# ScalarE in program order during the prologue, and w_in's magnitudes on VectorE, in a sigmoid-attention and MLP kernel

## The chip, the core and the metric

The kernel runs on one core of a Trainium2 chip. A core has five engines, each with an instruction stream of its own: TensorE (PE, matrix products; its weight loads are shown apart as PEld), VectorE (DVE), ScalarE (ACT), GpSimd (POOL) and SyncE (SP, which here only starts DMAs). An engine does its stream strictly in order; streams meet at semaphores. Data lies in SBUF (128 partitions), matrix products end in PSUM.

The metric is the time on the device of one execution, in microseconds (us). A profiled execution leaves a trace, with the begin and end of each instruction.

## The reference

```python
def _attn_ref(q, k, v):                      # each (8, 12, 448, 64), f32
    S = q.shape[2]
    scale = 1.0 / np.sqrt(q.shape[-1])
    scores = scale * np.matmul(q, k.transpose(0, 1, 3, 2)) - np.log(S)
    attn = 1.0 / (1.0 + np.exp(-scores))
    return np.matmul(attn, v).astype(np.float32)

def _moe_ref(x, w_in, w_out):                # (3584, 768) @ (768, 2048) @ (2048, 768)
    h = x @ w_in
    neg, pos = h <= -1.0, h >= 1.0
    g = np.where(pos, h, np.where(neg, 0.0, (h + 1.0) ** 2 / 4.0))
    return (g @ w_out).astype(np.float32)
```

The output of attention is put into x: one row for each of the 8 x 448 positions, 12 heads x 64 columns. Each weight of attention is a sigmoid by itself; there is no sum over a row.

## The kernel before

**Units of work.** A batch of 448 positions has 12 heads, taken two at a time: six pairs of heads a batch, 48 in all. A pair is four pieces, three of 128 key positions and a short one of 64, so a batch of attention is 24 pieces. `step(i)` does piece i: `scores` (products of k and q, L407 in the form of pairs 0 to 7), `weigh` (the sigmoid on ScalarE, L454 in batch 0 and 1, L457 later) and `av` (product with v, L498), which lags by three pieces. At the end of a pair ScalarE copies its x out of PSUM (L504) and VectorE takes the largest magnitude (L508).

**Number formats.** Products run in fp16, with each operand as a high and a low half and three products in place of one; a power of two, found from the largest magnitude, scales each operand first. Pairs 0 to 7 are an exception: they are used in f32 as they come. From pair 8 on, `load_pair` fetches a pair into one of two `raw` buffers, `prep_a` finds its largest magnitudes, and `prep_b` makes the scales and the halves. Up to pair 46 (`MAX_ACT = 47`) `prep_a` runs on ScalarE, three Abs passes that keep a sum (L344); after it on VectorE, two reductions (L346). Up to pair 16 (`QA = 17`) the halves come from ScalarE and VectorE (L373, L374), after it from GpSimd (L378 and the lines behind it).

**Weights.** w_in and w_out are 16 chunks of 128 rows each. They arrive as 64-bit words, whose bits `Weight.convert` turns into f32. For a chunk f these are, in order: an Abs pass on ScalarE (L224); the magnitudes; then on VectorE two shifts (L241), the low bits (L244) and the sign (L247). With chunk f's Abs go VectorE's lines for chunk f - 1 and, where a sum is used, the sum for chunk f - 2. Magnitudes come in two ways. For a chunk in `summed` (in w_in every second one) the values are only clamped (L226; on GpSimd below chunk 7, on VectorE from there), and ScalarE sums the converted chunk (L218). For the others VectorE clamps and keeps the largest value in one instruction (L236). w_in's raw words lie in room of w_out_sb until they are used, and the next load is issued from SP once a chunk is converted.

After chunks 0 to 7 `find_scale` makes w_in's first scale: a reduction, one product on TensorE that brings the largest value to all partitions (L175), and a few small instructions ending at L135 and L139 (in `scales`). `split` then makes the fp16 halves: high on ScalarE (L286), low on VectorE (L287). The halves of chunk f lie where the f32 values of chunk f - 1 were, so L286 of a chunk overwrites what L287 of the chunk before reads.

**Stages.** (1) The prologue: attention of batch 0 piece by piece, with the conversion of w_in woven in: 9 conversion steps by piece `WI_A = 14`, the rest after it. There the first scale is found and chunks 0 and 1 are split. Loads of pairs 8 and 9 are issued at pieces 9 and 12 (`L0`, `LSTEP`), their magnitudes at pieces 19 and 22 (`A0`). (2) `finish_x(0)`: the scale of batch 0's x and its halves, L521 and L522. (3) The up products of batch 0 (`ups`, L722, with `bend` at L735 to L739), half of its down products (L758), attention of batch 1, and the conversion of w_out. (4) Batch 1, in which w_in is also put together into blocks for a seven-product scheme (`mix`). (5) Batches 2 to 7: `ups_blocks` (L688), then `downs`, and in between attention of the next batch. An up phase and a down phase make one batch.

**What sets the order.** A scheduler sorts the instructions of each engine by a simulated timeline and by priority, in `high_priority` blocks earlier. An engine named in `manual_schedule` is left out of that: it takes its work in the order in which the program is written. Before, this holds for SP in the prologue's loop alone.

Of the kernel before, what the change touches and what calls it, by code (L numbers as in the profile page):

```python
# [14 lines left out]
F32 = mybir.dt.float32  # L15
# [3 lines left out]
AF = mybir.ActivationFunctionType  # L19
ALU = mybir.AluOpType  # L20
# [3 lines left out]
P = 128  # L24
# [12 lines left out]
NA = 8  # L37
AHEAD = 2
LAST = 84
LAST1 = 18  # L40
WI_A = 14
WI_B = 5
WO_A = 42
WO_B = 66
# [24 lines left out]

PM = 9  # L70
WI_PRIO = 280
X_PRIO = 593


@with_exitstack
def sigmoid_attention_mlp(ctx: ExitStack, tc: tile.TileContext, first_qvk, qkv, w_in, w_out, out_t):
    nc = tc.nc
    NFULL, _, _, S = first_qvk.shape
    B = out_t.shape[1] // S
    NFC, _, DM = w_out.shape  # L80
# [6 lines left out]
    GROUPS = slice(0, NA), slice(NA, NFC)  # L87
# [7 lines left out]
    out_p = ctx.enter_context(tc.tile_pool(name="outp", bufs=2))  # L95
# [4 lines left out]
    ps_mo = ctx.enter_context(tc.tile_pool(name="ps_mo", bufs=3, space=PSUM))  # L100
# [78 lines left out]
    class Weight:  # L179


        def __init__(self, dram, sb, name, spare):
            self.dram, self.sb, self.name, self.spare = dram.bitcast(I32), sb, name, spare
            self.words, self.at, self.loaded = {}, 0, 0
            self.scale, self.inv = [], []
            self.most = const.tile([P, 2, NFC], F32, name=name + "_most")
            nc.vector.memset(self.most, 0.0)
            mod = WI_SUM if name == "wi" else WO_SUM
            self.summed = [f for f in range(NFC) if mod and f % mod == 0 and f not in (NA - 1, NFC - 1)]

        def f32(self, f):
            return self.sb[:, f + 1].rearrange("p h n -> p (h n)").bitcast(F32)
# [16 lines left out]

        def convert(self):  # L210

            f = self.at - 2
            if 0 <= f < NFC:
                w = self.words.pop(f)
                if f in self.summed:

                    dump = wo.f32(-1) if self is wi else w[:, :DM].bitcast(F32)
                    nc.scalar.activation(dump, self.f32(f), AF.Abs, accum_out=self.most[:, 1, f : f + 1])  # L218
                if self is wo:
                    self.load(3 if f == 3 else 1)  # L220
            f = self.at
            if f < NFC:
                a = self.f32(f)
                nc.scalar.activation(a, self.words_of(f)[1].bitcast(F32), AF.Abs)  # L224
                if f in self.summed:
                    (nc.vector if f >= CLAMP else nc.gpsimd).tensor_scalar(  # L226
                        out=a, in0=a, scalar1=HIGH_MIN, scalar2=None, op0=ALU.max
                    )
            f = self.at - 1
            if 0 <= f < NFC:  # L230

                low, high = self.words_of(f)
                a = self.f32(f)
                ai = a.bitcast(I32)
                if f not in self.summed:
                    nc.vector.tensor_scalar(  # L236
                        out=a, in0=a, scalar1=HIGH_MIN, scalar2=0.0, op0=ALU.max, op1=ALU.max,
                        accum_out=self.most[:, 0, f : f + 1],
                    )

                nc.vector.tensor_scalar(  # L241
                    out=ai, in0=ai, scalar1=5, scalar2=2, op0=ALU.logical_shift_left, op1=ALU.logical_shift_right
                )
                nc.vector.scalar_tensor_tensor(  # L244
                    out=ai, in0=low, scalar=29, in1=ai, op0=ALU.logical_shift_right, op1=ALU.bitwise_or
                )
                nc.vector.scalar_tensor_tensor(  # L247
                    out=ai, in0=high, scalar=-0x40000000, in1=ai, op0=ALU.bitwise_and, op1=ALU.bitwise_or
                )
# [376 lines left out]
    def mix(i):  # L626
# [87 lines left out]
    hold = {}  # L714
# [28 lines left out]
    def down(b, m, u, k):  # L743

        lo, hi = (0, NFC) if k is None else (GROUPS[k].start, GROUPS[k].stop)
        if u == 0:
            hold["po"] = ps_mo.tile([P, 512], F32, tag="mo", name="po")
            hold["o"] = out_p.tile([P, S], F32, tag="o", name="o")
            if m == 0:
                hold["od"] = down_sc[b, k]()  # L750
            if k == 1:
                nc.sync.dma_start(out=hold["o"], in_=part[m])
        po, o = hold["po"], hold["o"]

        pair = (u, u + NFC // 2) if b >= SB else (lo + 2 * u, lo + 2 * u + 1)
        for f in pair:
# [137 lines left out]
    for b in range(1, B):  # L894
# [6 lines left out]
        first = at  # L901
# [65 lines left out]
```

## Time and the profile before

| | |
|---|---|
| three runs | 1194.42, 1192.86, 1188.74 us; median 1192.86 |
| profiled execution | 1187.38 us |
| its span in the trace, first to last instruction | 1185.7 us |
| busy in the span: PE, DVE, ACT, POOL | 1144.9, 854.9, 697.6, 332.8 us |
| first scale of w_in ready | 47.9 us |
| scale of batch 0's x ready | 90.0 us |
| first up product | 91.7 us |
| one batch from batch 2 on, from one first up product to the next | 137.2 us |

How to read it: a row of the timeline has its start and its duration in us, the engine, the line of the program, what is written from what, and in brackets how long the engine stood idle before, with what released it. A group's row has the busy time of its instructions, the mean duration of one in ns, and that idle time summed. A stretch's row (windows) has, for each engine, the busy time within the stretch and the number of instructions.

### The profile page before, as it was taken

Reading aid. Unit: us, or ns where it says so; the run is one execution under the profiler, and the core shown is the slowest. Engines: PE = TensorE matmul, PEld = TensorE weight load, DVE = VectorE, ACT = ScalarE, POOL = GpSimd, SP = SyncE. Lnnn points to the kernel's source line nnn. Section 1 sums busy time; section 2 is a strip of 40 time slices with the busy share of each in tenths; the row PEclk is TensorE's granted clock in tenths of the full one; section 3 lists DMA queues with packets and bytes.
Section 4 is the critical chain, followed back from the end, with each engine's and each line's share of the span. In section 5 each row is a group of like instructions: output and inputs, shape, how many; then the busy total and the mean of one; then the engine's idle time right before and its main releaser. Section 6 shows DMA issues by size and latency. Waiting matters only on the chain.

```text
span 1185.7 us, 20268 instructions
## 1 busy us (share of the span) xinstructions
PE 1144.9 (97%) x7662; PEld 669.3 (56%) x7662; DVE 854.9 (72%) x1828; ACT 697.6 (59%) x1158; POOL 332.8 (28%) x393
## 2 busy tenths in 40 slices
PE   5889899999999999999999999999999999999998
PEld 1224333444445776457754677557764577558954
DVE  6999999999956588457973689456884678736830
ACT  5886576665654577547864578455864476613510
POOL 3004410011323244234345235332532353310000
PEclk9899999999999999999999999999999999999999
DMA  9842354437542266224643065423552246302400
GB/s 367 322 153 76 118 161 152 134 119 257 182 148 72 95 217 210 76 72 142 238 163 102 30 236 208 135 64 128 204 211 64 65 147 220 126 24 87 163 16 32
DMA packets 58113, 170.01 MB, mean 143 GB/s; under 512 B 8608, under 2 KB 39840, under 8 KB 51872
## 3 DMA queue, kind: packets, MB, share of 16 engines
q1 hardware_dynamic: 56288, 159.29, 39.1%
q10 hardware_dynamic: 1728, 9.44, 2.2%
q8 instruction: 60, 0.98, 0.3%
q14 instruction: 37, 0.30, 0.1%
HBM read 126.94 MB, written 23.40 MB: 127 GB/s over the span
## 4 chain that ended last, share of the span: by engine, by line
PE 71%; DVE 17%; DMA 4%; ACT 3%; issue 2%; POOL 2%; SPq 0%; POOLq 0%; ACTq 0%; DVEq 0%
PE po L758 33%; PE ph L688 22%; PE pav L498 8%; PE psc L416 3%; PE psc L425 2%; PE ph L722 2%; DVE g L736 2%; PE psc L411 1%; DVE g L737 1%; DVE ghl L739 1%; DMA raw<-qkv 1%; DVE ahl L466 1%; DVE w_in_sb L244 1%; DVE mixa L632 1%; DVE w_out_sb L247 1%
## 5 line engine op out<-in xcount | busy, mean ns | idle before, releaser
L758 PE MATMUL po<-ghl,w_out_sb 128*128 128x448 f16 x2304 | 446.3, 353 | 1.5 <-DVE qkv_e L131 0.6
L758 PEld LDWEIGHTS <-w_out_sb 128*128 128x128 f16 x2304 | 221.7, 98 | 219.4 <-issue 15.9
L688 PE MATMUL ph<-w_in_sb 128*128 128x224 f16 x3024 | 307.7, 259 | 1.3 <-DVE g L737 0.9
L688 PEld LDWEIGHTS <-w_in_sb 128*128 128x128 f16 x3024 | 282.6, 98 | 30.1 <-issue 27.2
L466 DVE SCALAR_TENSOR_TENSOR ahl<-psc,ahl 128x896 f16<-128x896 f32 (+1 forms) x170 | 153.0, 900 | 105.7 <-ACT ahl L465 103.6
L378 POOL TENSOR_SCALAR raw<-raw,qkv_s 128x448 f32<-128x448 f32 (+1 forms) x93 | 71.0, 777 | 449.9 <-DVE qkv_i L139 346.3
L457 ACT ACTIVATE psc<-psc,nls,sqk 128x896 f32<-128x896 f32 (+1 forms) x136 | 129.5, 971 | 103.5 <-PE psc L425 86.6
L465 ACT ACTIVATE ahl<-psc 128x896 f16<-128x896 f32 (+1 forms) x170 | 126.9, 762 | 29.8 <-DVE ahl L466 28.6
L722 PE MATMUL ph<-xhl,w_in_sb 128*128 128x448 f16 x576 | 114.5, 356 | 4.7 <-DVE g L737 3.4
L344 ACT ACTIVATE dump<-raw 128x448 f16<-128x448 f32 (+1 forms) x105 | 61.9, 589 | 85.8 <-DMA raw<-qkv 84.5
L697 DVE TENSOR_TENSOR xhl<-ph,xhl 128x224 f32<-128x224 f32 x240 | 87.7, 383 | 25.3 <-PE ph L688 19.4
L738 ACT ACTIVATE ghl<-g 128x448 f16<-128x448 f32 x128 | 72.5, 573 | 44.2 <-DVE g L737 43.8
L498 PE MATMUL pav<-ahl,v 128*64 128x448 f16 x748 | 95.6, 360 | 0.0
L735 ACT ACTIVATE g<-xhl,hr,ihr 128x448 f32<-128x448 f32 x96 | 68.7, 752 | 41.9 <-DVE xhl L697 41.0
L722 PEld LDWEIGHTS <-w_in_sb 128*128 128x128 f16 x576 | 55.7, 99 | 63.6 <-issue 14.4
L736 DVE SCALAR_TENSOR_TENSOR g<-g,rk 128x448 f32<-128x448 f32 x112 | 81.4, 741 | 10.2 <-ACT g L735 10.0
L739 DVE TENSOR_TENSOR ghl<-g,ghl 128x448 f16<-128x448 f32 x128 | 85.0, 672 | 5.3 <-ACT ghl L738 4.8
L768 DVE TENSOR_SCALAR o<-po,od 128x448 f32<-128x448 f32 x48 | 32.5, 679 | 61.1 <-PE po L758 60.8
L380 POOL TENSOR_TENSOR hl<-raw,hl 128x448 f16<-128x448 f32 x62 | 71.1, 1167 | 0.0
L416 PE MATMUL psc<-qk 128*128 128x448 f16 x252 | 66.3, 354 | 2.0 <-ACT a L454 1.0
L737 DVE SCALAR_TENSOR_TENSOR g<-xhl,ihs,g 128x448 f32<-128x448 f32 x96 | 66.3, 708 | 0.3
L498 PEld LDWEIGHTS <-v 128*64 128x64 f16 x748 | 36.3, 109 | 37.9 <-issue 23.0
(167 smaller groups left out, 1198.5 us busy)
## 6 DMA issues: line engine op xcount, KB each, us to landing
w_in_sb<-blocks SPq DMA_DIRECT2D x48, 1344.0 KB, 6.1
raw<-qkv SPq DMA_DIRECT2D x34, 704.0 KB, 4.7
qk<-hl SPq DMA_DIRECT2D x320, 56.0 KB, 2.0
w_out_sb<-w_in SPq DMA_DIRECT2D x16, 768.0 KB, 8.5
out_t<-o SPq DMA_DIRECT2D x48, 224.0 KB, 1.9
blocks<-mixs SPq DMA_DIRECT2D x8, 768.0 KB, 3.5
w_out_sb<-w_out ACTq DMA_DIRECT2D x6, 768.0 KB, 4.1
raww<-w_out ACTq DMA_DIRECT2D x6, 768.0 KB, 5.7
```

Of the source, the lines that this page charges most:

```text
L416: nc.tensor.matmul(out, kq[:, j, 1, w], kq[:, j, 0, :], start=True, stop=False)
L457: nc.scalar.activation(a, a, AF.Sigmoid, bias=nls, scale=sqk)
L465: nc.scalar.activation(hi, x, AF.Copy, scale=ATT)
L466: nc.vector.scalar_tensor_tensor(out=lo, in0=x, scalar=ATT, in1=hi, op0=ALU.mult, op1=ALU.subtract)
L498: nc.tensor.matmul(pav[j * D : (j + 1) * D, :S], *terms[j][t], start=c == 0 and t == 0, stop=mid and t == len(terms[j]) - 1,)
L688: nc.tensor.matmul(out, w[:, wt, wh, c * P : (c + 1) * P], xc[:, xt, c, xh, :], start=j in (0, 2) and c + wh + xh == 0, stop=c == HC - 1 a ...
L697: add = lambda out, q, other: nc.vector.tensor_tensor(out=out, in0=quarter(q), in1=other, op=ALU.add)
L722: nc.tensor.matmul(ph[:, :S], w_in_sb[:, f, wh, c * P : (c + 1) * P], xhl[:, c, xh, :], start=c == 0 and wh + xh == 0, stop=c == NCC - 1 a ...
L736: nc.vector.scalar_tensor_tensor(out=g, in0=g, scalar=rt, in1=g, op0=ALU.min, op1=ALU.mult)
L737: nc.vector.scalar_tensor_tensor(out=g, in0=h, scalar=ihs, in1=g, op0=ALU.mult, op1=ALU.max)
L739: (nc.gpsimd if f % GPOOL else nc.vector).tensor_tensor(out=ghl[:, f, 1, :], in0=g, in1=hi, op=ALU.subtract)
L758: nc.tensor.matmul(po[:, :S], w_out_sb[:, f, wh, m * P : (m + 1) * P], ghl[:, f, gh, :], start=f == lo and wh + gh == 0, stop=f == hi - 1 ...
```

## The change

It consists of constants and a few lines:

- `AM = 1`: in the prologue's loop ScalarE, too, takes its work in program order.
- `WI_SUM = 0`: `summed` is empty. The 8 sums on ScalarE (L218) and the 8 clamps (L226, four on GpSimd and four on VectorE) are gone; L236, now L240, runs on all 16 chunks of w_in. `CLAMP` and `SLAG` then have nothing to act on.
- `WI_A = 11`: the first nine conversion steps are spread over 11 pieces instead of 14, and the scale of w_in and the first two splits come after piece 11.
- `MAX_ACT = 20`: the magnitudes of pairs 20 to 46 come from VectorE (now L350, two instructions a pair) instead of ScalarE (three).
- `QA = 20`: the halves of pairs 17 to 19 are made by ScalarE and VectorE instead of GpSimd.
- `L0 = 10`, `LSTEP = 1`: loads of pairs 8 and 9 at pieces 10 and 11, magnitudes at 19 and 20.
- `X_PRIO = 600`: a priority, for `finish_x(0)`.
- `MIXA = 0`, `CUT = 8` and the keys of `hold`: new switches, left where they give the instructions and the order of before.

Lines of the program move by three or four (L135 becomes L138, L454 becomes L458), behind `mix` by seven (L722 becomes L729).

```diff
-WI_A = 14
+WI_A = 11
-WI_SUM = 2
-WO_SUM = 0
-MAX_ACT = 47
-L0 = 9
+WI_SUM = 0
+MAX_ACT = 20
+L0 = 10
-LSTEP = 3
+LSTEP = 1
-CLAMP = 7
-QA = 17
+CLAMP = 2
+QA = 20
+SLAG = 2
+AM = 1
+MIXA = 0
+CUT = 8
-X_PRIO = 593
+X_PRIO = 600
...
-            mod = WI_SUM if name == "wi" else WO_SUM
-            self.summed = [f for f in range(NFC) if mod and f % mod == 0 and f not in (NA - 1, NFC - 1)]
+            mod = WI_SUM if name == "wi" else 0
+            early = [f for g in GROUPS for f in range(g.start, g.stop - SLAG + 1)]
+            self.summed = [f for f in early if mod and f % mod == 0]
...
+            f = self.at - SLAG
+            if 0 <= f < NFC and f in self.summed:
+                nc.scalar.activation(wo.f32(-1), self.f32(f), AF.Abs, accum_out=self.most[:, 1, f : f + 1])
             f = self.at - 2
             if 0 <= f < NFC:
-                w = self.words.pop(f)
-                if f in self.summed:
-                    dump = wo.f32(-1) if self is wi else w[:, :DM].bitcast(F32)
-                    nc.scalar.activation(dump, self.f32(f), AF.Abs, accum_out=self.most[:, 1, f : f + 1])
+                self.words.pop(f)
...
-    with tc.manual_schedule(engines={mybir.EngineType.SP}):
+    with tc.manual_schedule(engines={mybir.EngineType.SP} | ({mybir.EngineType.Activation} if AM else set())):
```

Some instructions move with this. The first place is the start of ScalarE's stream. `a_123` and the other a are sigmoids of batch 0's pieces in turn, `w_in_sb<-w_out_sb` is the Abs of a chunk of w_in. Before:

```order
L224 ACT_TABLE_LOAD
L224 ACTIVATE w_in_sb<-w_out_sb 128x768
L454 ACT_TABLE_LOAD
L454 ACTIVATE a_123<-psc,nls 128x896
L454 ACTIVATE a_128<-psc,nls 128x896
L224 ACTIVATE w_in_sb<-w_out_sb 128x768
L218 ACTIVATE w_out_sb,wi_most<-w_in_sb 128x768
L224 ACTIVATE w_in_sb<-w_out_sb 128x768
L454 ACTIVATE a_133<-psc,nls 128x896
L454 ACTIVATE a_140<-psc,nls 128x448
```

ScalarE in the changed kernel, from its start:

```order
L458 ACT_TABLE_LOAD
L458 ACTIVATE a_123<-psc,nls 128x896
L458 ACTIVATE a_128<-psc,nls 128x896
L458 ACTIVATE a_133<-psc,nls 128x896
L458 ACTIVATE a_140<-psc,nls 128x448
L458 ACTIVATE a_149<-psc,nls 128x896
L228 ACTIVATE w_in_sb<-w_out_sb 128x768
L458 ACTIVATE a_157<-psc,nls 128x896
L228 ACTIVATE w_in_sb<-w_out_sb 128x768
```

The first Abs stands behind five sigmoids instead of ahead of all, and one table load is gone with it.

The second place is VectorE behind w_in's first scale (`wi_s`, and its inverse `wi_i`). L287, now L291, is the low half of a split; L236, now L240, the largest value; L241 and L244, now L245 and L248, belong to the conversion. Before:

```order
L135 TENSOR_SCALAR wi_s<-wi_e 128x1
L139 TENSOR_SCALAR wi_i<-wi_e 128x1
L135 TENSOR_SCALAR qkv_s<-qkv_e 128x2
L139 TENSOR_SCALAR qkv_i<-qkv_e 128x2
L156 CAST mb<-m_447 128x2
L241 TENSOR_SCALAR w_in_sb<-w_in_sb 128x768
L360 TENSOR_SCALAR sqk<-qkv_i 128x1
L244 SCALAR_TENSOR_TENSOR w_in_sb<-w_out_sb,w_in_sb 128x768
L247 SCALAR_TENSOR_TENSOR w_in_sb<-w_out_sb,w_in_sb 128x768
L287 SCALAR_TENSOR_TENSOR w_in_sb<-w_in_sb,wi_s 128x768
```

VectorE in the changed kernel at the same place:

```order
L138 TENSOR_SCALAR wi_s<-wi_e 128x1
L142 TENSOR_SCALAR wi_i<-wi_e 128x1
L291 SCALAR_TENSOR_TENSOR w_in_sb<-w_in_sb,wi_s 128x768 x2
L512 TENSOR_REDUCE xm<-x_91 128x1
L291 SCALAR_TENSOR_TENSOR w_in_sb<-w_in_sb,wi_s 128x768 x2
L240 TENSOR_SCALAR w_in_sb,wi_most<-w_in_sb 128x768
L291 SCALAR_TENSOR_TENSOR w_in_sb<-w_in_sb,wi_s 128x768
L245 TENSOR_SCALAR w_in_sb<-w_in_sb 128x768
L240 TENSOR_SCALAR w_in_sb,wi_most<-w_in_sb 128x768
L248 SCALAR_TENSOR_TENSOR w_in_sb<-w_out_sb,w_in_sb 128x768
L291 SCALAR_TENSOR_TENSOR w_in_sb<-w_in_sb,wi_s 128x768
```

Splits have come forward, right behind the scale, and the scales of pair 8 (`qkv_s`) have gone back. On ScalarE the high halves (L290) come at the same place, two and two, with sigmoids of batch 0 and a copy of x (L508) between them:

```order
L290 ACTIVATE w_in_sb<-w_in_sb,wi_s 128x768 x2
L458 ACTIVATE a_308<-psc,nls 128x896
L508 ACTIVATE x_91<-pav 128x448
L458 ACTIVATE a_319<-psc,nls 128x448
L290 ACTIVATE w_in_sb<-w_in_sb,wi_s 128x768 x2
L458 ACTIVATE a_327<-psc,nls 128x896
L228 ACTIVATE w_in_sb<-w_out_sb 128x768
```

Before, sigmoids, conversions and splits stood there one and one in turn.

The third place is VectorE in an up phase of a later batch, in the changed kernel. L743 and L744 are `bend`, L704 adds products of the blocks, `m_7899` holds the largest magnitudes of a pair that has been loaded:

```order
L743 SCALAR_TENSOR_TENSOR g<-g,rk_6801 128x448
L350 TENSOR_REDUCE m_7899<-raw 128x2
L350 TENSOR_REDUCE m_7899<-raw 128x1
L743 SCALAR_TENSOR_TENSOR g<-g,rk_6791 128x448
L704 TENSOR_TENSOR xhl<-ph,xhl 128x224
L744 SCALAR_TENSOR_TENSOR g<-xhl,ihs_6805,g 128x448
L470 SCALAR_TENSOR_TENSOR ahl<-psc,ahl 64x448
L159 CAST mb<-m_7899 128x3
```

The two reductions are new there; before, three Abs passes on ScalarE (L344) did this work, and VectorE's stream held the same rows without them.

More of the change, by code (lines that the diff above doesn't have):

```diff
@@ L654, in mix @@
             for h in range(2):
-                nc.vector.tensor_scalar(
-                    out=pv[:, h, t0 : t0 + n, :], in0=src[:, h], scalar1=to[k], scalar2=None, op0=ALU.mult
-                )
+                if MIXA:
+                    nc.scalar.activation(pv[:, h, t0 : t0 + n, :], src[:, h], AF.Copy, scale=to[k])
+                else:
+                    nc.vector.tensor_scalar(
+                        out=pv[:, h, t0 : t0 + n, :], in0=src[:, h], scalar1=to[k], scalar2=None, op0=ALU.mult
+                    )
         nc.sync.dma_start(out=blocks[i][:, : 3 * DM], in_=pl)
@@ L746, in down @@
         if u == 0:
-            hold["po"] = ps_mo.tile([P, 512], F32, tag="mo", name="po")
-            hold["o"] = out_p.tile([P, S], F32, tag="o", name="o")
+            hold["po", m] = ps_mo.tile([P, 512], F32, tag="mo", name="po")
+            hold["o", m] = out_p.tile([P, S], F32, tag="o", name="o")
             if m == 0:
@@ L751, in down @@
             if k == 1:
-                nc.sync.dma_start(out=hold["o"], in_=part[m])
-        po, o = hold["po"], hold["o"]
+                nc.sync.dma_start(out=hold["o", m], in_=part[m])
+        po, o = hold["po", m], hold["o", m]
         pair = (u, u + NFC // 2) if b >= SB else (lo + 2 * u, lo + 2 * u + 1)
@@ L788, in downs @@
         n = NFC if k is None else GROUPS[k].stop - GROUPS[k].start
-        return [lambda m=m, u=u: down(b, m, u, k) for m in range(NCC) for u in range(n // 2)]
+        order = [(m, u) for m in range(NCC) for u in range(n // 2)]
+        if b >= SB:
+            first = [(m, u) for m in range(2) for u in range(CUT)] + [(m, u) for m in range(2) for u in range(CUT, n // 2)]
+            order[: n] = first
+        return [lambda m=m, u=u: down(b, m, u, k) for m, u in order]
     def step(i):
```

## The prediction

> **What bounds the kernel now.** The page's 40 slices come first, then the stretches. Slices are 29.6 us wide.
>
> ```profile
> PE   5889899999999999999999999999999999999998
> DVE  6999999999956588457973689456884678736830
> ```
> ```profile
> 20.00:40.00 20.00, 12.81 (x42) 3.20 (x41) 19.86 (x31) 12.65 (x22) 4.25 (x2) 0.74 1.03 405
> 60.00:80.00 20.00, 15.59 (x68) 4.25 (x68) 20.00 (x34) 17.97 (x25) 0.00 (x0) 1.00 0.61 208
> 92.00:205.00 113.00, 107.22 (x535) 44.28 (x534) 107.47 (x211) 76.52 (x120) 30.01 (x22) 1.00 0.37 121
> 205.00:330.00 125.00, 120.03 (x647) 57.79 (x646) 118.02 (x244) 80.23 (x127) 19.71 (x19) 0.99 0.51 172
> 500.00:600.00 100.00, 100.00 (x802) 69.45 (x800) 75.90 (x181) 66.42 (x114) 40.65 (x51) 1.00 0.45 154
> ```
>
> In a stretch stand its length, then the busy times of TensorE (PE), its weight loads, VectorE (DVE), ScalarE (ACT) and GpSimd. There are two regimes. From about 330 us on TensorE is full and nothing else ends a wait for long. Ahead of that VectorE is: 20.00 of 20 us at 60, 95% from 92 to 205 and 94% to 330. Between 20 and 80 TensorE idles, but it waits for an order that VectorE sets. So the prologue must be read on VectorE: work added there, or a wait put in front of it, moves the first up matmul and, since VectorE stays full behind it, nearly all that follows. Four moments mark the path: VectorE's first piece of w_in, w_in's first scale, the scale of batch 0's x, and the first up matmul.
>
> ```profile
> 11.21 0.56 DVE L241 TENSOR_SCALAR w_in_sb<-w_in_sb 128x768 int32<-128x768 int32 x1 [10.13 <-POOL w_in_sb L226]
> 47.87 0.14 DVE L135 TENSOR_SCALAR wi_s<-wi_e 128x1 int32<-128x1 int32 x1
> 89.99 0.15 DVE L135 TENSOR_SCALAR x_s<-x_e 128x1 int32<-128x1 int32 x1
> 91.74 1.53 PE L722 MATMUL ph<-xhl,w_in_sb 128*128 128x448 f16 x7
> ```
>
> Behind the x scale the order of VectorE's instructions is the same in both kernels for some 200 rows, so I add up what reaches that scale later.
>
> **The change part by part.**
>
> **1. VectorE starts later: +4.0 us.** Before, ScalarE takes w_in's first chunk as soon as it lands (8.07). Now five sigmoids stand ahead of it, so pieces 0 to 4 must be scored first.
>
> ```profile
> 4.46 3.35 PE L407 MATMUL psc<-ghl 64*128 64x448 f32 x8 [4.46 <-DMA ghl<-first_qvk]
> 8.07 0.89 ACT L224 ACTIVATE w_in_sb<-w_out_sb 128x768 f32<-128x768 f32 x1 [5.99 <-DMA w_out_sb<-w_in]
> 13.12 1.76 PE L498 MATMUL pav<-a,ghl 128*64 128x448 f32 x4
> 17.14 1.02 PE L407 MATMUL psc<-ghl 64*128 64x448 f32 x4
> 18.10 0.97 PE L498 MATMUL pav<-a,ghl 128*64 128x448 f32 x4
> ```
> ```profile
> L454 ACT ACTIVATE a<-psc,nls 128x896 f32<-128x896 f32 x24 | 24.1, 1008 | 4.2 <-PE psc L407 4.1
> L224 ACT ACTIVATE w_in_sb<-w_out_sb 128x768 f32<-128x768 f32 x16 | 14.6, 911 | 7.4 <-DMA w_out_sb<-w_in 7.4
> ```
>
> Scores 0 and 1 end at 4.46 + 3.35 = 7.8. Scores 2 to 4 and two value products follow: at the fast pace (1.02 and 0.97) 5.0 us, at the slow one of 13.12 some 9. I take 5.4, since TensorE no longer pauses and should soon be fast: 13.2, then a sigmoid of 1.0 and the magnitude pass of 0.9: VectorE starts at 15.2 instead of 11.2. Ends: 14.5 and 18 (+3.3, +7). The table load that goes (one of two) lies in ScalarE's idle time.
>
> **2. More work on VectorE: +5.1 us.** With all maxima on VectorE, L236 runs 16 times on w_in instead of 8, and the four clamps L226 on VectorE go.
>
> ```profile
> 32.04 0.96 DVE L244 SCALAR_TENSOR_TENSOR w_in_sb<-w_out_sb,w_in_sb 128x768 int32<-128x768 int32 x1
> 32.91 0.95 DVE L236 TENSOR_SCALAR_CACHE_REDUCE w_in_sb<-w_in_sb 128x768 f32<-128x768 f32 x1
> 33.78 0.95 DVE L247 SCALAR_TENSOR_TENSOR w_in_sb<-w_out_sb,w_in_sb 128x768 int32<-128x768 int32 x1
> 34.65 0.56 DVE L241 TENSOR_SCALAR w_in_sb<-w_in_sb 128x768 int32<-128x768 int32 x1
> 35.12 0.55 DVE L226 TENSOR_SCALAR w_in_sb<-w_in_sb 128x768 f32<-128x768 f32 x1
> 35.59 0.95 DVE L244 SCALAR_TENSOR_TENSOR w_in_sb<-w_out_sb,w_in_sb 128x768 int32<-128x768 int32 x1
> ```
>
> Independent instructions overlap a little, so starts are what counts: L236 takes 33.78 - 32.91 = 0.87, L226 0.47. 8 x 0.87 - 4 x 0.47 = 5.1; by full durations (0.95 + 0.08, 0.56) 6.0. No cover hides it, VectorE being full. The eight sums that ScalarE loses (L218) free no one on the path: ScalarE had waited for VectorE there.
>
> **3. Splits one behind another: +5.7 us.** Once w_in's scale is known, VectorE's next rows are now L291 x2, a maximum, L291 x2, where before two conversions and other work lay between such rows. Each takes what ScalarE's L290 has just made, and L290 of the next chunk overwrites what L291 of the one before still reads; this wait stands once in the trace of before:
>
> ```profile
> 77.27 0.93 ACT L286 ACTIVATE w_in_sb<-w_in_sb,wi_s 128x768 f16<-128x768 f32 x1 [1.77 <-DVE w_in_sb L287]
> L287 DVE SCALAR_TENSOR_TENSOR w_in_sb<-w_in_sb,wi_s 128x768 f16<-128x768 f32 x9 | 9.2, 1020 | 0.2 <-ACT w_in_sb L286 0.2
> ```
>
> So the two engines take turns, and VectorE idles some 1.05 us (0.93 and the signal) for each of the first two, 0.55 for the copy of x behind the second, then about 1.0 for each of the next three, between which ScalarE in its written order does sigmoids and a magnitude pass: 2.1 + 0.55 + 3.0 = 5.65. Below, 0 would need rows between them, which the order shows there are not enough of; above, 8 if the later splits wait too.
>
> **4. GpSimd's clamps go: -2.6 us.** They made VectorE wait 0.5 us behind the start, and five of its instructions were long while GpSimd worked; the first and the last:
>
> ```profile
> 16.25 1.46 DVE L247 SCALAR_TENSOR_TENSOR w_in_sb<-w_out_sb,w_in_sb 128x768 int32<-128x768 int32 x1
> 27.31 0.98 DVE L241 TENSOR_SCALAR w_in_sb<-w_in_sb 128x768 int32<-128x768 int32 x1
> 15.62 2.58 POOL L226 TENSOR_SCALAR w_in_sb<-w_in_sb 128x768 f32<-128x768 f32 x1 [4.44 <-ACT w_in_sb L224]
> ```
>
> Against 0.96 and 0.56 that is 0.50 and 0.42; I take 2.1 for the five (five at 0.42), so -2.6; bounds -2.0 and -3.0. The Trainium skill (GPSIMD Engine Reference, 1. Specifications) has it that GpSimd shares its SBUF interfaces with VectorE and is in contention with VectorE instructions of two SBUF inputs or in a two-port mode; the two rows agree. By that page's 8. Key points VectorE is structurally about twice as fast at elementwise work, which would make taking the clamp off GpSimd a plain gain; that is the rival below in which the start is what counted.
>
> **Sum to the first up matmul: 4.0 + 5.1 + 5.7 - 2.6 = +12.2 us**, at 104 instead of 91.7. On the SP queue the loads of w_in's later chunks wait for VectorE's conversions and shift with them; pair 4's load stands behind one more of these, which matters only at piece 16; the loads of pairs 8 and 9 (now at 10 and 11 instead of 9 and 12) are wanted 10 pieces later. I cost these at nothing; were one late, it would be a landing of some us more.
>
> **5. Splits of pairs 17 to 19 on ScalarE and VectorE.** 2 x 0.68 + 0.76 us each on VectorE, while GpSimd gets about 11 us less each. Pair 17's falls at 313 us into a full VectorE, the other two behind 330 where it has room.
>
> ```profile
> L374 DVE SCALAR_TENSOR_TENSOR hl<-raw,qkv_s,hl 128x448 f16<-128x448 f32 x6 | 4.0, 680 | 0.3 <-ACT hl L373 0.3
> L374 DVE SCALAR_TENSOR_TENSOR v<-raw,qkv_s,v 128x512 f16<-128x512 f32 x3 | 2.3, 755 | 0.0
> 312.79 2.06 POOL L378 TENSOR_SCALAR raw<-raw,qkv_s 128x448 f32<-128x448 f32 x3 [24.88 <-issue]
> ```
>
> Ends -1 (less contention) and +2.1; I take +1.
>
> **6. Magnitudes of 27 pairs from ScalarE to VectorE: 0.** That is 1.09 + 0.68 = 1.8 us more on VectorE for each, about 13 of them in the up phases, where it is fullest. One pair did so before already, and had to wait for its load as well:
>
> ```profile
> 985.47 1.09 DVE L346 TENSOR_REDUCE m<-raw 128x2 f32<-128x896 f32 x1 [2.74 <-DMA raw<-qkv]
> 990.42 1.89 PE L688 MATMUL ph<-w_in_sb 128*128 128x224 f16 x18 [0.36 <-DVE xhl L697]
> 1006.00 0.35 PE L416 MATMUL psc<-qk 128*128 128x448 f16 x1 [0.40 <-issue]
> ```
>
> A delay of 2.74 + 1.8 = 4.5 us cost TensorE 0.76. So it bears about 3.7, and 1.8 without the wait should cost nothing. In an up phase before, a pair's load was issued at 587.65 and landed 4.2 later, 591.85; VectorE reaches the new place at about 590 plus its delay, so the wait is 2 us at most. Bounds: 0 and 13 x 0.76 = 9.9, and -1 for ScalarE's own waits:
>
> ```profile
> ACT dump L344 <- DMA raw<-qkv: 81.9, 14, 8.6
> ```
>
> In the down phases VectorE waited for those very magnitudes before, so there the wait only changes its row. Nothing comes of new buffer keys in the down loop, of CUT = 8 (the same order) or of MIXA = 0.
>
> **Sum: 12.2 + 1 + 0 = +13.2 us.** The profiled execution took 1187.38; with it 1200.6. The median of the runs shown, 1192.86, lies 5.5 above that execution, and they spread over 5.7; I put the sum on the median: 1206.
>
> **The rivals.**
> - **The start and the order matter, VectorE's load doesn't: faster.** In the prologue TensorE waited for sigmoids that stood behind other work on ScalarE:
>
> ```profile
> PE psc L407 <- ACT a L454: 14.4, 7, 3.5
> ```
>
> If program order ended these waits and the 5.1 us alone came back, the time would be 1192.9 - 14.4 + 5.1 = 1183.6. It decides if the x scale comes before 89.99. Against it: its maximum stands behind some 120 rows of VectorE, full from 20 us on. Chance 0.10.
> - **The turns cost little.** If ScalarE is ahead enough and TensorE and VectorE take up part of the shift later, 5 us are left: 1198. Chance 0.22.
> - **VectorE inherits ScalarE's waits for loads, in the up phases.** 13 x 0.76 on top: 1216. For it: up-phase slices with VectorE at 9; against it: the landing before. Chance 0.13.
>
> **How the numbers follow.** Forecast 0.55: 1206, its own range 1199 to 1214. Leaving out most of the fast rival and the far end of the last, 1192 to 1219 holds eight in ten. A measurement can tell about 0.5% (6 us) from no change. Slower by more: 0.55 + 0.13 + a few of the second rival, 0.71; within: the rest of that one, 0.18; faster: 0.11.
>
> **What would show it.** VectorE's first L240 near 15; the w_in scale near 47 as before; behind it five waits of L291 for L290, some 5 us; the x scale near 102 and L729 near 104. From batch 2 on a batch should still take 137 us. It would be wrong if the x scale came by 90 us, or if the batches grew or shrank by more than 1 us each.

## The result, and the profile after

| | before | changed |
|---|---|---|
| median | 1190.8 us (4 runs, 1188.32 to 1194.42) | 1206.24 us (4 runs, 1206.17 to 1207.84) |
| ratio | | 1.0137, 95% interval 1.0115 to 1.0159 |
| profiled execution, its span | 1187.38, 1185.7 | 1206.17, 1204.5 |
| busy PE, DVE, ACT, POOL | 1144.9, 854.9, 697.6, 332.8 | 1144.8, 911.5, 648.5, 296.9 |

The changed kernel is 1.4% slower. Of e1, one execution ran at a granted clock of 0.75 throughout and took 1470.71 us, so the marks of that kernel below come from e5, the same kernel at a granted clock of 0.986.

The four moments of the prediction, with the turns behind w_in's scale, from VectorE's timeline of the changed kernel:

```profile
14.19 0.95 DVE L240 TENSOR_SCALAR_CACHE_REDUCE w_in_sb<-w_in_sb 128x768 f32<-128x768 f32 x1 [13.11 <-ACT w_in_sb L228]
...
45.39 0.15 DVE L138 TENSOR_SCALAR wi_s<-wi_e 128x1 int32<-128x1 int32 x1
...
46.55 1.02 DVE L291 SCALAR_TENSOR_TENSOR w_in_sb<-w_in_sb,wi_s 128x768 f16<-128x768 f32 x1 [0.94 <-ACT w_in_sb L290]
48.57 1.02 DVE L291 SCALAR_TENSOR_TENSOR w_in_sb<-w_in_sb,wi_s 128x768 f16<-128x768 f32 x1 [1.00 <-ACT w_in_sb L290]
49.90 0.62 DVE L512 TENSOR_REDUCE xm<-x 128x1 f32<-128x448 f32 x1 [0.31 <-ACT x L508]
51.24 1.02 DVE L291 SCALAR_TENSOR_TENSOR w_in_sb<-w_in_sb,wi_s 128x768 f16<-128x768 f32 x1 [0.73 <-ACT w_in_sb L290]
53.27 1.02 DVE L291 SCALAR_TENSOR_TENSOR w_in_sb<-w_in_sb,wi_s 128x768 f16<-128x768 f32 x1 [1.00 <-ACT w_in_sb L290]
54.94 0.95 DVE L240 TENSOR_SCALAR_CACHE_REDUCE w_in_sb<-w_in_sb 128x768 f32<-128x768 f32 x1 [0.66 <-ACT w_in_sb L228]
...
101.24 0.15 DVE L138 TENSOR_SCALAR x_s<-x_e 128x1 int32<-128x1 int32 x1
```

and from TensorE's:

```profile
102.99 7.07 PE L729 MATMUL ph<-xhl,w_in_sb 128*128 128x448 f16 x36
```

VectorE's start is 2.98 later, the x scale and the first up product 11.25. In brackets stand the waits in the place where the prediction had its turns: 0.94 + 1.00 + 0.31 + 0.73 + 1.00 + 0.66 = 4.64 us in which VectorE waits for ScalarE.

The stretches give the rest. For each kernel three follow: from VectorE's first piece of w_in to the x scale, from the same piece to the first up product of batch 2, and from that to the last one of batch 7 (columns: length, then busy PE, PEld, DVE, ACT, POOL, the clock, DMA). Before:

```profile
11.21:89.99 78.78, 62.57 (x236) 16.27 (x236) 76.97 (x138) 62.54 (x93) 6.83 (x3) 0.89 0.75 280
11.21:394.40 383.19, 356.18 (x1787) 151.22 (x1787) 336.19 (x681) 248.15 (x388) 75.46 (x68) 0.97 0.48 167
394.40:1131.40 737.00, 734.77 (x5602) 490.88 (x5601) 510.00 (x1129) 442.45 (x764) 254.52 (x318) 1.00 0.40 138
```

Changed:

```profile
14.19:101.24 87.05, 56.44 (x208) 15.62 (x208) 81.16 (x151) 52.66 (x72) 0.00 (x0) 0.78 0.66 238
14.19:407.80 393.61, 352.44 (x1759) 150.43 (x1759) 346.20 (x706) 239.53 (x364) 46.10 (x38) 0.94 0.47 160
407.80:1150.20 742.40, 732.05 (x5603) 489.73 (x5602) 556.53 (x1179) 399.79 (x614) 250.06 (x318) 1.00 0.40 137
```

This is VectorE's account. To the x scale: start +2.98, busy 81.16 - 76.97 = +4.19, not busy 5.89 - 1.81 = +4.08, together +11.25. To batch 2: start +2.98, busy +10.0, not busy +0.4, together +13.4. An account of this kind always adds up, and it says where a shift arises only while the engine is full. In the last 64.4 us ahead of batch 2 VectorE has room in both kernels and TensorE has none, so nothing is lost there, although VectorE does 7.8 us more (before, then changed):

```profile
330.00:394.40 64.40, 64.40 (x365) 32.22 (x362) 32.26 (x84) 26.91 (x46) 18.91 (x24) 1.00 0.32 102
343.40:407.80 64.40, 64.40 (x362) 31.88 (x359) 40.03 (x96) 26.75 (x41) 5.11 (x6) 1.00 0.32 102
```

Without that stretch the account reads: start +2.98, busy +2.2, not busy +8.2, the same 13.4 together. So most of the shift is time in which VectorE stands idle, half of it ahead of the x scale and half behind. The batches then take 5.4 longer, and 13.4 + 5.4 = 18.8 is the whole difference of the two spans. The two medians lie closer, 15.4 apart, since the profiled execution of before is one of its quickest.

A wait that the prediction did not name stands on ScalarE (timeline of the changed kernel):

```profile
30.73 0.92 ACT L228 ACTIVATE w_in_sb<-w_out_sb 128x768 f32<-128x768 f32 x1 [0.65 <-DMA w_out_sb<-w_in]
45.58 0.93 ACT L290 ACTIVATE w_in_sb<-w_in_sb,wi_s 128x768 f16<-128x768 f32 x1 [13.93 <-DVE wi_s L138]
```

In its written order the first split stands behind piece 11 and ahead of later sigmoids. It waits 13.93 us for w_in's scale, and all attention stands still meanwhile. So there are two readings. **VectorE theory:** the shift is made by VectorE's later start, its added work and its turns with ScalarE. **ScalarE rival:** ScalarE's standing still makes the pieces late, and VectorE's rows only follow.

### The profile page after: what moved, and what is told of

Same layout as the page of the kernel before. It is cut to its first block, busy times and chain, and to the rows that moved or that the text cites. A ratio compares the mean times of both kernels' runs of the same rounds, so it can differ in the third digit from the quotient of the medians.

```text
span 1204.5 us, 20113 instructions
## 1 busy us (share of the span) xinstructions
PE 1144.8 (95%) x7662; PEld 669.3 (56%) x7662; DVE 911.5 (76%) x1903; ACT 648.5 (54%) x988; POOL 296.9 (25%) x362
## 4 chain that ended last, share of the span: by engine, by line
PE 57%; DVE 24%; DMA 7%; issue 4%; ACT 4%; POOL 3%; SPq 1%; ACTq 0%; POOLq 0%; DVEq 0%
PE po L765 29%; PE ph L695 14%; PE pav L502 6%; DMA raw<-qkv 3%; DVE g L744 3%; DVE g L743 3%; PE ph L729 3%; PE psc L420 3%; DVE ahl L470 3%; PE psc L429 2%; DVE ghl L746 2%; DVE xhl L704 1%; DVE w_in_sb L240 1%; DVE w_in_sb L248 1%; DVE m L350 1%
## 5 line engine op out<-in xcount | busy, mean ns | idle before, releaser
L382 POOL TENSOR_SCALAR raw<-raw,qkv_s 128x448 f32<-128x448 f32 (+1 forms) x84 | 59.5, 725 | 401.0 <-issue 269.9
L729 PE MATMUL ph<-xhl,w_in_sb 128*128 128x448 f16 x576 | 114.6, 356 | 4.0 <-DVE g L744 2.5
L704 DVE TENSOR_TENSOR xhl<-ph,xhl 128x224 f32<-128x224 f32 x240 | 87.1, 381 | 19.0 <-PE ph L695 15.5
L743 DVE SCALAR_TENSOR_TENSOR g<-g,rk 128x448 f32<-128x448 f32 x112 | 86.9, 785 | 5.1 <-ACT g L742 5.1
L729 PEld LDWEIGHTS <-w_in_sb 128*128 128x128 f16 x576 | 55.6, 99 | 63.2 <-issue 14.2
L746 DVE TENSOR_TENSOR ghl<-g,ghl 128x448 f16<-128x448 f32 x128 | 80.9, 641 | 5.3 <-ACT ghl L745 4.9
L350 DVE TENSOR_REDUCE m<-raw 128x2 f32<-128x896 f32 (+1 forms) x56 | 46.9, 877 | 38.6 <-DMA raw<-qkv 38.5
L744 DVE SCALAR_TENSOR_TENSOR g<-xhl,ihs,g 128x448 f32<-128x448 f32 x96 | 74.8, 793 | 0.1
L384 POOL TENSOR_TENSOR hl<-raw,hl 128x448 f16<-128x448 f32 x56 | 61.1, 1113 | 0.0
L441 POOL COPY w_in_sb<-hl 64x128 f16<-64x128 f16 x68 | 31.7, 467 | 116.4 <-DVE hl L378 114.4
```

The source lines that it names most:

```text
L704: add = lambda out, q, other: nc.vector.tensor_tensor(out=out, in0=quarter(q), in1=other, op=ALU.add)
L729: nc.tensor.matmul(ph[:, :S], w_in_sb[:, f, wh, c * P : (c + 1) * P], xhl[:, c, xh, :], start=c == 0 and wh + xh == 0, stop=c == NCC - 1 a ...
L743: nc.vector.scalar_tensor_tensor(out=g, in0=g, scalar=rt, in1=g, op0=ALU.min, op1=ALU.mult)
L744: nc.vector.scalar_tensor_tensor(out=g, in0=h, scalar=ihs, in1=g, op0=ALU.mult, op1=ALU.max)
L746: (nc.gpsimd if f % GPOOL else nc.vector).tensor_tensor(out=ghl[:, f, 1, :], in0=g, in1=hi, op=ALU.subtract)
```

## The experiments

Twelve experiments, of which e1 and e5 are the same kernel (its time from e1, its marks from e5). The kernel before had medians of 1190.41 (beside e1 to e4), 1189.38 (e5 to e8) and 1190.98 us (e9 to e12), with single runs from 1185.37 to 1194.98. The columns: median; ratio to before, with its interval; VectorE's first piece of w_in; the x scale; the first up product of batch 2; batches 2 to 7 from first to last up product; whether the 27 pairs' magnitudes are on VectorE.

| | median | ratio | start | x scale | batch 2 | batches | mags |
|---|---|---|---|---|---|---|---|
| before | | 1 | 11.2 | 90.0 | 394.4 | 737.0 | no |
| changed | 1206.24 | 1.0137 (1.0115 to 1.0159) | 14.2 | 101.2 | 407.8 | 742.4 | yes |
| e1, e5 | 1212.49 | 1.0178 (1.0142 to 1.0215) | 9.6 | 90.5 | 415.2 | 741.5 | yes |
| e2 | 1214.33 | 1.0203 (1.0167 to 1.0239) | 16.7 | 108.2 | 415.1 | 742.4 | yes |
| e3 | 1204.69 | 1.0127 (1.0093 to 1.0160) | 14.4 | 99.3 | 403.7 | 743.8 | yes |
| e4 | 1203.22 | 1.0110 (1.0078 to 1.0143) | 14.9 | 102.5 | 408.9 | 735.5 | no |
| e6 | 1206.20 | 1.0139 (1.0122 to 1.0156) | 16.4 | 104.3 | 413.9 | 737.1 | no |
| e7 | 1196.76 | 1.0064 (1.0049 to 1.0079) | 8.3 | 89.2 | 404.8 | 735.4 | no |
| e8 | 1197.00 | 1.0060 (1.0045 to 1.0075) | 12.3 | 90.4 | 395.5 | 743.4 | yes |
| e9 | 1200.63 | 1.0085 (1.0052 to 1.0118) | 9.6 | 100.8 | 407.2 | 737.9 | no |
| e10 | 1204.98 | 1.0120 (1.0092 to 1.0147) | 8.8 | 94.0 | 412.6 | 736.8 | no |
| e11 | 1190.71 | 1.0005 (0.9986 to 1.0023) | 10.0 | 90.4 | 398.2 | 736.8 | no |
| e12 | 1192.14 | 1.0011 (0.9996 to 1.0026) | 9.9 | 89.1 | 396.5 | 737.4 | no |

A mark comes from one execution each, and single executions of before differ by several us; so of a few us of difference the intervals decide.

**e1 and e5: ScalarE sorted again.**

```diff
-AM = 1
+AM = 0
```

> The changed kernel with ScalarE sorted by the scheduler again (AM = 0), all else as changed. Marks of the changed kernel: first piece of w_in on VectorE 14.2, w_in scale 45.4, x scale 101.2, first up product 103.0, span 1204.5. VectorE theory (the shift is VectorE's own ledger: later start, more work, turns with ScalarE at the splits): the start comes back to 11.2 (-3.0), the turns behind the w_in scale go (-4.6), the extra maxima stay: x scale about 93.6, time about 1198.6. ScalarE rival (the shift is made by ScalarE standing still behind rows that wait, which starves the attention pieces): all of it goes, x scale about 90, time about 1195.

> The kernel of e1 once more, for a profile at full clock. Its times lay 6 us above the changed kernel though its first up product came at 93.3 instead of 103.0, so some 16 us must be lost behind it. VectorE theory: fewer of VectorE's rows stand ahead of the x scale, they return between 93 and 330 us, and TensorE waits there for bend (L743 to L745) or for w_in's second scale (113 us, 20 us behind the first up product; 13 in the kernel before). ScalarE rival: the batches from 400 us on get longer, since ScalarE's order there is another one; the up products of batch 2 then start 10 us earlier than in the changed kernel, and the loss comes behind.

The x scale came back to 90.5, with 1.2 us of waits of VectorE on the way, and still the time did not fall: its median lies some 5 us above the changed kernel's, though the two intervals overlap. Both theories missed that. From the first up product (92.3) to batch 2 it took 322.9 us, against 302.7 before and 304.8 changed. One stretch, of e5 and then of the changed kernel:

```profile
150.00:175.00 25.00, 18.53 (x77) 7.98 (x76) 24.48 (x56) 12.11 (x22) 0.24 (x1) 0.80 0.32 107
150.00:175.00 25.00, 22.43 (x107) 8.32 (x104) 25.00 (x47) 16.52 (x27) 2.97 (x4) 0.93 0.45 143
```

At 150 VectorE is about as full, but TensorE gets 18.5 us of work out of 25 instead of 22.4, and the clock that it is granted is 0.80. The expectation had it that VectorE does here what it had not done ahead of the x scale. The traces speak against that: ahead of the x scale the groups of VectorE's rows have the same counts in e5 as in the changed kernel (but for one of 0.1 us), and from the first up product to batch 2 its work is nearly the same (e5, then changed):

```profile
92.31:415.17 322.86, 299.91 (x1542) 136.19 (x1540) 265.43 (x549) 184.54 (x288) 42.18 (x38) 0.96 0.39 129
102.99:407.80 304.81, 294.29 (x1545) 134.30 (x1543) 263.89 (x550) 185.24 (x290) 46.10 (x38) 0.99 0.41 137
```

Of the 18 us more TensorE is idle for 12.4 and busy for 5.6, with as many products at a lower granted clock. Its waits for `bend` (L744) ahead of up products rise from 2.5 to 9.6 us, as the expectation had it. So the amount of VectorE's work is not the reason. Its order differs: conversions of w_out stand between the halves of x (L526, from 92.16 to 97.68; in the changed kernel 102.73 to 106.88 without them), and w_in's second scale comes 17.3 us behind the first up product (109.62 against 92.31), and 13.2 us behind it in the changed kernel. That this order is the cause is argued; no run tried it by itself. An early x scale, at any rate, is no gain by itself. The expectation's other branch, longer batches, fell: 741.5.

**e2: sums back on ScalarE.**

```diff
-WI_SUM = 0
+WI_SUM = 2
-CLAMP = 2
+CLAMP = 7
```

> The changed kernel with every second chunk of w_in summed on ScalarE and clamped on GpSimd or VectorE again (WI_SUM = 2, CLAMP = 7). VectorE theory: 5.1 us of work leaves VectorE, 2.3 us of GpSimd's contention comes back: x scale about 98.4 instead of 101.2, time about 1203.4. ScalarE rival: x scale stays at 101 or comes later, since ScalarE gets eight sums more in its fixed order; time 1206 or above.

x scale 108.2, the time 0.7% above the changed kernel: the rival's side, in a direction that the VectorE theory had excluded. ScalarE's timeline shows the price of a sum in a fixed order (L219 is the former L218):

```profile
28.21 0.84 ACT L219 ACTIVATE w_out_sb<-w_in_sb 128x768 f32<-128x768 f32 x1 [4.08 <-DVE w_in_sb L251]
...
36.68 0.84 ACT L219 ACTIVATE w_out_sb<-w_in_sb 128x768 f32<-128x768 f32 x1 [4.11 <-DVE w_in_sb L251]
...
44.73 0.84 ACT L219 ACTIVATE w_out_sb<-w_in_sb 128x768 f32<-128x768 f32 x1 [3.73 <-DVE w_in_sb L251]
```

Each waits some 4 us for VectorE to finish a chunk. The next chunk's Abs stands behind it, so VectorE runs dry in its turn. In VectorE's account to batch 2, e2 has 5.1 us less work than the changed kernel (341.1 against 346.2), 2.5 us of later start and 9.9 us more not busy; the last 64.4 us are the same in both.

**e3: the first two splits written four pieces later.**

```diff
                 with tc.high_priority(offset=WI_PRIO):
                     wi.find_scale()
+            if at == WI_A + 4:
+                with tc.high_priority(offset=WI_PRIO):
                     wi.split(0)
                     wi.split(1)
```

> The changed kernel with the first two splits of w_in written four pieces later than its scale, so that sigmoids stand ahead of them in ScalarE's program order and it need not stand still 13.9 us for the scale. VectorE theory: only the turns go, 4.6 us of idle time of VectorE behind the scale; x scale about 96.6, time about 1201.6. ScalarE rival: the 13.9 us stall was what made the pieces late; x scale about 90 to 92, time about 1196.

ScalarE's stop for the scale shrank from 13.93 to 7.86 us, and the x scale came 2.0 earlier. The rival's 10 us did not come. VectorE's waits on the way went from 5.1 to 3.6 only, so its theory's 4.6 did not come either. In time e3 differs from the changed kernel by less than the intervals.

**e4 and e8: magnitudes, taken back and taken alone.**

```diff
-MAX_ACT = 20
+MAX_ACT = 47
```

> The changed kernel with the magnitudes of pairs 20 to 46 on ScalarE again (MAX_ACT = 47). As the prediction had it (no cost): span 1204.5 and time 1206, no change. By the trace of the changed kernel (batches 2 to 7 took 742.4 us from first to last up product instead of 737.0, with 6.4 us of TensorE waiting for VectorE's L704): the marks up to the first up product stay, and those 5.4 us go; time about 1200.8.

e8 is the kernel before with the opposite edit, `MAX_ACT = 47` to `20`:

> The kernel before with the magnitudes of pairs 20 to 46 on VectorE (MAX_ACT = 20) and nothing else of the change. As the prediction had it: no change, time as before. By e4 (batches 2 to 7 took 735.5 us from first to last up product without it, 742.4 with it): x scale 90, batches 737.0 become about 743, time some 6 us above before.

e4's median lies 3.0 us below the changed kernel's, which by the intervals is not clear of no change. e8 is clear: alone the magnitudes made the kernel 0.60% slower (1197.0 against 1189.38). In the table the column "batches" falls into two groups by this edit and nothing else: 741.5 to 743.8 with them on VectorE, 735.4 to 737.9 without. The waits of TensorE in the batches say for what. Before:

```profile
PE ph L688 <- DVE xhl L697: 0.4, 1, 0.4
```

e8, with the magnitudes alone (the numbers are us in total, times, the longest):

```profile
PE ph L688 <- DVE xhl L697: 6.2, 10, 0.7
```

Changed:

```profile
PE ph L695 <- DVE xhl L704: 6.4, 11, 0.7
```

They stand at the same two places of a batch, 138.1 us apart from batch to batch where before a batch took 137.2 (TensorE's timeline, changed):

```profile
465.43 2.75 PE L695 MATMUL ph<-w_in_sb 128*128 128x224 f16 x27 [0.60 <-DVE xhl L704]
472.37 2.56 PE L695 MATMUL ph<-w_in_sb 128*128 128x224 f16 x25 [0.69 <-DVE xhl L704]
...
603.55 2.75 PE L695 MATMUL ph<-w_in_sb 128*128 128x224 f16 x27 [0.60 <-DVE xhl L704]
...
610.48 2.56 PE L695 MATMUL ph<-w_in_sb 128*128 128x224 f16 x25 [0.69 <-DVE xhl L704]
```

and VectorE's rows of the magnitudes ahead of the last two of these, again changed:

```profile
588.33 1.68 DVE L350 TENSOR_REDUCE m<-raw 128x2 f32<-128x896 f32 x2 [0.67 <-DMA raw<-qkv]
...
605.54 1.66 DVE L350 TENSOR_REDUCE m<-raw 128x2 f32<-128x896 f32 x2
607.13 0.67 DVE L743 SCALAR_TENSOR_TENSOR g<-g,rk 128x448 f32<-128x448 f32 x1
607.73 0.37 DVE L704 TENSOR_TENSOR xhl<-ph,xhl 128x224 f32<-128x224 f32 x1
```

From 588.33 on VectorE's timeline has no gap up to both waits. The first pair waited 0.67 us for its load, the second (no bracket) for nothing. What delays L704, for which TensorE waits, is above all the 1.7 us of work in a queue that was full already.

**e6 and e7: two parts alone.** e6 is the kernel before with ScalarE in program order:

```diff
-    with tc.manual_schedule(engines={mybir.EngineType.SP}):
+    with tc.manual_schedule(engines={mybir.EngineType.SP, mybir.EngineType.Activation}):
```

> The kernel before with ScalarE in program order during the prologue and nothing else of the change. VectorE theory (order of ScalarE costs by the start, the sums that wait for VectorE and the splits): start at 14 to 17 instead of 11.2, turns of 3 to 5 us: x scale 97 to 100 instead of 90.0, time about 1199. ScalarE rival (the program order is all of the shift, and the new maxima are no cost): x scale 101 or later, time 1202 to 1208. Both fall if the x scale stays within 2 us of 90.

e7 is the kernel before with all maxima on VectorE:

```diff
-WI_SUM = 2
+WI_SUM = 0
```

> The kernel before with all maxima of w_in on VectorE (WI_SUM = 0) and nothing else of the change. VectorE theory: 5.1 us more work, 2.3 less contention with GpSimd, 0.5 less wait: x scale 92.3 instead of 90.0, time 2 us above before. ScalarE rival: no cost, or a gain, as ScalarE loses eight sums: x scale 90 or earlier.

The order alone costs 16.8 us, as much as the whole change. The x scale of 104.3 and the time lie where the ScalarE rival had them, and later than the VectorE theory allowed. VectorE's waits up to its first up product, in e6:

```profile
DVE w_in_sb L241 <- POOL w_in_sb L226: 15.6, 2, 15.4
DVE w_in_sb L226 <- ACT w_in_sb L224: 4.0, 2, 3.7
DVE xm L508 <- ACT x L504: 2.3, 1, 2.3
```

It starts at 16.4, behind the late Abs and GpSimd's clamp, and then waits for ScalarE. In its account to batch 2 e6 has +5.2 start, no more work and +14.4 not busy.

The maxima alone cost 7.4 us, not 2: the x scale came at 89.2, as the rival had it, and then it went as in e5. From the first up product to batch 2, before and then e7:

```profile
91.74:394.40 302.66, 291.91 (x1545) 134.46 (x1543) 258.01 (x537) 183.92 (x293) 68.63 (x65) 0.99 0.42 138
90.46:404.76 314.30, 293.92 (x1541) 135.52 (x1540) 258.04 (x537) 182.46 (x291) 67.00 (x65) 0.97 0.40 132
```

VectorE has the same 537 instructions and 258.0 us of work there, and TensorE is idle for 9.6 us more. Batch 2 began 10.4 us late, and TensorE's waits between 92 and 330 us show 8.6 us for VectorE's L737 and 4.5 for L522, where before had 3.4 and 0.4.

So the parts don't add: 16.8 + 7.4 + 7.6 (e8) = 31.8, and the change has 15.4. Maxima on VectorE cost 7.4 us beside a sorted ScalarE, but save some 8 beside one in program order (1.0203 against 1.0137), since the sums that made it wait are gone. The order costs 16.8 alone, and beside the change's other parts it costs nothing that can be seen: 1.0137 with it, 1.0178 without, with intervals that overlap.

**e9 and e10: the start, and the stop for the scale.** Both build on e4. e9 writes the Abs of chunk 0 behind the first sigmoid, and e10 in addition the two splits nine pieces behind the scale:

```diff
         for i in range(LAG):
             scores([i])
+            if i == 0:
+                convert(wi, 1)
```

> The kernel of e4 (the changed kernel with the magnitudes back on ScalarE) with the Abs of w_in's chunk 0 written behind the first sigmoid instead of behind the fifth. Marks of e4: VectorE's first piece of w_in 14.9, x scale 102.5, up products of batch 2 from 408.9, to 1144.4. VectorE theory: it starts at about 9.5 and has chunk 0 (3.4 us of work) done before chunk 1 comes: x scale some 3 us earlier, 99.5, batch 2 from about 406. ScalarE rival: the next sigmoids come up to 2 us later, so the x scale stays at 102 or comes later.

> The kernel of e9 with the first two splits written nine pieces behind w_in's scale (nearly at the prologue's end), so that nothing in ScalarE's program order waits for that scale early. VectorE theory: of VectorE's 5.1 us of idle time before the x scale the turns behind the w_in scale go, some 4: x scale 95 to 96, batch 2 from about 402. ScalarE rival: its 13.9 us stall was what counted, so 10 us or more come back: x scale 90 or earlier and batch 2 from 396 or earlier, as in the kernel before.

e9: VectorE starts 5.2 earlier, but its timeline shows the next thing that is late:

```profile
17.17 0.95 DVE L240 TENSOR_SCALAR_CACHE_REDUCE w_in_sb<-w_in_sb 128x768 f32<-128x768 f32 x1 [3.98 <-ACT w_in_sb L228]
```

chunk 1's Abs. The x scale gains 1.75, and the intervals of e4 and e9 overlap. e10: without the stop the x scale comes 6.8 earlier than in e9, nearer the VectorE theory's 95 to 96 than the rival's 90. But batch 2 begins 5.4 later (412.6 against 407.2) and the median rises by 4.4 us (four runs from 1203.92 to 1205.85, against 1199.61 to 1202.75): the pattern of e5 and e7. ScalarE's 13.9 us stop, the most striking wait of the changed kernel, was no loss that moving the splits gave back.

**e11 and e12: a version faster than both?** e11 takes chunk 0 out of the summed chunks, and e12 puts all clamps on VectorE, both in the kernel before:

```diff
-            self.summed = [f for f in range(NFC) if mod and f % mod == 0 and f not in (NA - 1, NFC - 1)]
+            self.summed = [f for f in range(NFC) if mod and f and f % mod == 0 and f not in (NA - 1, NFC - 1)]
```

> The kernel before with chunk 0 of w_in taken out of the summed chunks: its maximum comes from VectorE (L236), so VectorE need not wait for GpSimd's clamp (10.1 us at the start). VectorE's rows behind chunk 0 keep their order. VectorE theory: start at about 8.5 to 9 instead of 11.2, 0.87 us more work: x scale and batch 2 some 1.5 to 2 us earlier, time 1187 to 1188. Rival (the start is hidden by waits for ScalarE and the loads behind it): no change, or 0.9 us slower.

```diff
-CLAMP = 7
+CLAMP = 0
```

> The kernel before with all eight clamps (L226) on VectorE (CLAMP = 0), so that GpSimd has none. VectorE theory: four clamps more, 1.9 us; the contention (2.1 to 2.4) and the waits for GpSimd (0.5) go, and the start comes about 1.5 to 2 us earlier: 2 to 3 us faster, time 1187. Rival: the scheduler's new order of VectorE pushes work behind the x scale as in e7, which gave 10 us at batch 2's start back: 5 us or more slower.

No difference either way, at intervals of 0.2%. VectorE started 1.3 us earlier in both; nothing of it reached the end. None of the twelve beats the kernel before.

So neither reading carries through the prologue. e2 and e6 came out on the ScalarE rival's side; e3 and e10 took its stop away in part or whole, and what it promised did not come. The VectorE theory missed e1, e2, e3, e6, e7, e11 and e12; in e10 its x scale was nearly met, but not what should follow from it. What the magnitudes cost in the batches is shown.

## Why the prediction came out, point by point

- **Start, +4.0:** measured +2.98. TensorE kept its fast pace from 8.6 us on, so the scores ahead of the first Abs took less than the 5.4 us allowed for them. As a price it was read too high: in e9 an earlier start of 5.2 gave 1.75, in e11 and e12 1.3 gave nothing, as the next Abs or the next chunk ends the gain.
- **Work, +5.1, and contention, -2.6:** VectorE's busy time to the x scale rose by 4.19, where 5.1 - 2.1 = 3.0 had been counted as busy. The part of GpSimd shows in the groups of that stretch, before:

```profile
L247 DVE SCALAR_TENSOR_TENSOR w_in_sb<-w_out_sb,w_in_sb 128x768 int32<-128x768 int32 x16 | 16.0, 1001 | 0.2
L244 DVE SCALAR_TENSOR_TENSOR w_in_sb<-w_out_sb,w_in_sb 128x768 int32<-128x768 int32 x16 | 15.8, 989 | 0.2
L241 DVE TENSOR_SCALAR w_in_sb<-w_in_sb 128x768 int32<-128x768 int32 x16 | 9.7, 609 | 10.7 <-POOL w_in_sb L226 10.7
```

and changed:

```profile
L248 DVE SCALAR_TENSOR_TENSOR w_in_sb<-w_out_sb,w_in_sb 128x768 int32<-128x768 int32 x16 | 15.2, 952 | 0.1
L251 DVE SCALAR_TENSOR_TENSOR w_in_sb<-w_out_sb,w_in_sb 128x768 int32<-128x768 int32 x16 | 15.1, 952 | 0.1
...
L245 DVE TENSOR_SCALAR w_in_sb<-w_in_sb 128x768 int32<-128x768 int32 x16 | 8.8, 556 | 0.2
```

  41.5 - 39.1 = 2.4 us for the same 48 instructions: the estimate of 2.1 held. e12, the kernel before without GpSimd's clamps, has 39.5 for them, which shows the cause.
- **Turns, +5.7:** 4.64 in the place forecast: four waits of L291 where five were forecast, one of the maximum, and one of L240.
- **Sum to the first up product, +12.2:** measured +11.25. Measured less forecast, the parts are -1.0 (start), +1.2 (busy, against 3.0) and -1.1 (not busy, 4.08 against 5.2), so they cancel in part. To batch 2 it was 13.2 with pair 17's split, measured 13.4. The shift of VectorE's maxima of x (L508, now L512) is 11.8 us at 303.57 and 13.75 at 330.78, and pair 17's rows (L378) stand between, from 326.88. That fits their 2.0 us, but it was not tried by itself.
- **Magnitudes, 0: this is the term that was mis-sized.** It stood in the step "1.8 without the wait should cost nothing", drawn from one place where a delay of 4.5 us had cost TensorE 0.76. Measured: +5.4 in the changed kernel, which is 0.9 a batch and just inside the prediction's own sign of being wrong, and 0.60% alone in e8. That place was at 985 us, in one batch; the new rows stand in the fullest part of every up phase, and there 1.7 us of work cost TensorE some 0.6 us twice a batch. The rival of inherited load waits priced 9.9 and had the right engine and phase, but not the main cause: the loads add 0.67 us at one of the two places.
- **The level.** The sum was put on a median of 1192.86, from three runs; later medians of before were 1189.4 to 1191.0. So the forecast of 1206 and the measured 1206.24 agree closer than the working does: the missing cost of the magnitudes and a level 2 us or more too high cancel in part. Against its own profiled execution the sum gave 1200.6, and the changed kernel's took 1206.17, 5.6 more; the 5.5 put on top to come to the median happened to fill that gap. That 1206 was met to the microsecond is luck; that the kernel is slower by more than 1%, mostly ahead of batch 2, is not.
- **What the steps could not tell:** they price the edits one by one on the trace of before. "The eight sums that ScalarE loses free no one on the path" was right there, but e2 shows that beside ScalarE's new order their removal is what keeps the loss at 15 us instead of 24. The sum came out because it was made on the changed order as a whole (the rows of VectorE up to the x scale), not from prices of single edits. Its terms up to the x scale are found in the trace of the changed kernel, but no run that took one of them away (e1 and e5, e3, e9, e10) gave it back as time clear of the intervals, so as causes of the 15.4 us they are argued and not shown.

Left open: which engine sets the prologue's shift; what in the order behind an early x scale costs the time up to batch 2 (18.1 us more in e5 than in the changed kernel, 11.6 more in e7 than before); the splits of pairs 17 to 19 by themselves; and why single runs of before spread over 10 us.

## What to carry to other kernels

- While an engine is full over several stages, take its account (start, busy, not busy) up to the point where it stops being full, and no further: 64 us more turned +2.2 busy and +8.2 not busy into +10.0 and +0.4. A mark inside the stretch, such as the first product of the next stage, can come 11 us earlier and the end no earlier (e5).
- In program order, an instruction that waits for another engine holds up all that is written behind it. Look for those that wait for a whole chunk (the sums, the first split), and price them together with the order: the maxima cost 7.4 us alone and saved some 8 beside the order.
- Spare time that a trace shows at one place of a phase is not spare time of the phase: 1.7 us of work, put at two full places of a batch, cost 0.9 us in each of six batches.

## What the runs showed of the hardware

TensorE is slow for a while after a long pause. Its timeline of the changed kernel, with products of equal shape ahead of and behind the pause of 31.7 to 49.5 us (in which one product of 0.27 us ran):

```profile
17.18 1.02 PE L411 MATMUL psc<-ghl 64*128 64x448 f32 x4 [0.27 <-ACT a L458]
18.14 2.48 PE L502 MATMUL pav<-a,ghl 128*64 128x448 f32 x12
...
49.48 1.86 PE L411 MATMUL psc<-ghl 64*128 64x448 f32 x4 [5.25 <-ACT a L458]
51.27 4.62 PE L502 MATMUL pav<-a,ghl 128*64 128x448 f32 x12
55.82 1.02 PE L411 MATMUL psc<-ghl 64*128 64x448 f32 x4
```

1.86 instead of 1.02 and 4.62 instead of 2.48, for some 6 us; the granted clock from 49.48 to 55.80 was 0.51. So this stop of ScalarE cost TensorE 3.0 us beyond its length. The Trainium skill (TensorE: Matmul & The Clock Gate, Part 1: The HAM clock gate) has it that the array falls to half rate after an idle window of about 3.4 us and comes back after at least one such window of sustained work. These rows come near the ratio (1.8 and 1.9), and the slow phase here lasted nearer two such windows than one.
